# Cross-shaped window attention on one core: 34 squares by VectorE's f16 product, and a new mix of tile kinds

## The chip, the cores and the metric

One of the eight cores of a Trainium2 chip runs the kernel. Its engines work side by side, each from an instruction queue of its own, and wait for each other by semaphores: TensorE (PE) multiplies matrices into PSUM, ScalarE (ACT) and VectorE (DVE) read PSUM and SBUF, GpSimd (POOL) reads and writes SBUF, SyncE (SP) issues transfers. The metric is the time of one execution on the device in microseconds; less is better.

## The reference

An image x of 224 x 224 positions with 96 channels is projected to queries, keys and values. The first 48 channels attend within horizontal stripes of 8 rows (28 windows of 1792 tokens), the last 48 within vertical stripes of 8 columns (28 windows more). The two results side by side go through an output projection.

```python
qkv = jnp.einsum('bhwc,cd->bhwd', x, wqkv)
q, k, v = (qkv[..., :C].copy(), qkv[..., C:2 * C].copy(), qkv[..., 2 * C:].copy())
scale = C2 ** (-0.5)                              # C2 = 48
qh = q[..., :C2].reshape(B * nh, sw * W, C2)      # horizontal stripes; kh, vh alike
ah = _softmax(jnp.einsum('bqc,bkc->bqk', qh, kh) * scale, axis=-1)
oh = jnp.einsum('bqk,bkc->bqc', ah, vh).reshape(B, H, W, C2)
...
# qv, kv, vv: the other 48 channels in vertical stripes, ov likewise
o = jnp.pad(oh, ...) + jnp.pad(ov, ...)
return jnp.einsum('bhwc,cd->bhwd', o, wo)
```

## The kernel before, in words

**Tiles.** The 56 windows are worked off in 28 pairs P, 14 horizontal and then 14 vertical; the two windows of a pair lie in the two halves of the 128 partitions. A pair's 1792 queries are cut into four chunks c (512, 512, 512 and 256). The keys go along the partitions. One tile is 128 x 1024 scores: 1024 columns are two blocks of 64 keys by 512 queries, for two windows (in the last chunk four blocks by 256 queries). There are 14 tiles for each chunk of 512 and 7 for the last, 49 for a pair, 1372 in all. A tile's scores come from `score_half` (L768: four matmuls of 512 columns, or eight of 256), its exponentials are written as 16-bit words into one of 33 buffers PT, and `pv_fn` (L791) multiplies these with the values and adds the products up in a PSUM bank. The first product uses the diagonal 64 x 64 quadrants of the PE array and the second the other two, so matmuls of the two run side by side in pairs.

**Kinds.** Four engines share the exponentials, and the table KINDS says for each P and c what kind its last tiles are:

- E (not written in the table): ScalarE takes the exponential of the whole tile out of two PSUM banks (L947, `emit_qk`).
- Q, two passes: VectorE makes a f16 word from the low 16 bits of the scores, in two halves (L1037, `emit_p`, "p1"); GpSimd squares the whole tile (L1046, `squared`, kind "T"); PE computes the scores a second time into other banks, and VectorE adds score and square to the word whose bits are a bf16 (L1039, "f").
- H, four words: VectorE makes one word from the scores with one addition, in two halves (L1035), and GpSimd makes three shifted copies of it in three further PT buffers (L1051, `shifted`, kind "S"). All four words are multiplied with values, the three copies with values that GpSimd weighted before (V2, L1056), so an H tile costs four products L791 where the other kinds cost one.

Q and H tiles use a ring of four PSUM banks, together with the projections' results; E tiles use two fixed sets of two banks.

**Order.** The order of PE's work is written out by hand in ORDER, a string of letters for each P: q is scores and exponential of an E tile, 1 and x the two halves of a Q or H tile's first scores, 2 and y those of the second scores (3 both halves of a first one), v one product with the values, k, f, g and j parts of projections. While the program is built, a planner walks through these letters with a cost for each operation (D_H, D_SQ, D_AF and so on, in us) and decides from them in which order VectorE (`dve_step`) and GpSimd (`pool_step`) take the work that is ready. What it decides is fixed in each engine's queue; at run time semaphores alone hold an instruction back. VectorE also empties all projections and finished sums out of PSUM (L599, L608, L643, L711, L967), and GpSimd also normalises (L1022) and weights the values.

The lines of the three steps of a Q tile:

```python
lambda e: e.tensor_scalar(y.bitcast(FP16), l, YA ** 0.5 / 65536.0, -YA ** 0.5 * YD, ALU.mult, ALU.add)  # p1
return ("T", D_SQ, lambda e: e.tensor_tensor(y, y, y, ALU.mult), yk + ["pser"], yk)                      # squared
lambda e: e.scalar_tensor_tensor(y.bitcast(U16), f, QK, y.bitcast(FP16), ALU.add, ALU.add)               # f
```

Of the kernel before, what the change touches and what calls it, by code (L numbers as in the profile page):

```python
# [12 lines left out]
ALU = mybir.AluOpType  # L13
# [3 lines left out]
PHASE = 192.5  # L17
YA, YD = 43.12396, 0.0085264
QK, HK = -8394.91455, 5086.5133 + 128.0 * (85.205091 - 192.5)
SHIFTS = [32, 64, 96]  # L20
# [3 lines left out]
    ["QHH", "HHQQ", "QH", ""],  # L24
    ["HQQH", "HQ", "HQQHQ", ""],
    ["QHHHQQ", "HQQQ", "QQH", ""],
    ["HHQH", "QQ", "HQQHQQH", ""],
    ["HQHQQQH", "Q", "HHQH", ""],
    ["QHQQQ", "HQHQQ", "HQHHQQ", ""],
    ["HHQQQ", "QQQQ", "QH", ""],  # L30
    ["HQQHQ", "HQ", "HHQ", ""],
    ["QQQHHQH", "QQQQQHH", "", ""],
    ["HQQQHH", "HQQQQH", "QHH", ""],
    ["Q", "HQQQHQ", "QHQ", ""],
    ["HHQQHQQ", "QQQQH", "H", ""],
    ["HQQHQQH", "QQQHH", "", ""],
    ["HQQQHQ", "HQQQHQ", "H", ""],
    ["HHQQQQQ", "QHQ", "HH", ""],
    ["HQHQQQH", "QQQ", "HH", ""],
    ["HQHQHQ", "HQQQ", "HQ", ""],  # L40
    ["HHQQ", "HQHQHQ", "QQ", ""],
    ["HHQHQQ", "HQ", "HHQQ", ""],
    ["HHQQH", "HQQ", "HHQ", ""],
    ["QHHQQ", "HQQHQQ", "H", ""],
    ["HQHQHQQ", "HQHQ", "QH", ""],
    ["HHQQHQ", "H", "HQQQHQ", ""],
    ["HHQHQ", "HQQHHQ", "", ""],
    ["HQQH", "QHHQHQ", "QH", ""],
    ["HQHQQ", "H", "HHQQH", ""],
    ["QQHQHQ", "QHHQQH", "Q", ""],  # L50
    ["QHQHQH", "HQQQQ", "HH", ""],
# [10 lines left out]
SEMD, SEMP, SELF, SEMX = 0.14, 0.11, 0.19, 0.03  # L62
# [4 lines left out]
D_H, D_F, D_SQ, D_AF = 0.599, 1.132, 1.851, 1.01  # L67
D_AW, D_AG, D_TS = 2.088, 1.127, 0.009
# [11 lines left out]
    "qqkjkqjkqjkq1qxjq1qx1kqjkqjkjq2vxvqyvkqvjkvjq1vvxkqvjkvqjkvjq1vkvqjkvjvqxv1vqkvxvjq1vvqxv1vqvxvqkv1vqjv2qvvxvyqv1vqv2vyqvxvq2vvyqvkvqjvkqv1jvqvkxvqjkvjq1vkvqjvxvqv1xvqv2vkq",  # L80
    "vj1vqvvyqvxvqv1xvqvvkqjkvjqvk1vqjxvvqv1kqvjxvqv1vxvqkv2jqvyvv1qkvjqvx1vqvkvqvxjvqv1vqxvv1q2vvxqvyvqv2v1qvyvqxvvkqvjvqv12vqvyvqvxkvqjkvjqkv2qjvvyqvk1qj2vvqxv1vqxvq1vvyqvvqvx1vq",
    "xvqvv1xqvkjqvkvjqvk1vqjkvjqvxv2qvkvyjqv1vxqv2vvq1xvvq1vvyqkvjqxv2vqvkvqjyvqv2vqyvv1qvv2qvxv1qvvyqv2vyvq2vvqxvkqjkvqjkvjq1vxqvvyvqkv1vqxvjqv1xvqkvjqv1xvqv1vqvvxq1vvq",
    "vxv1qvxqvkvjq2vv1qvkvjqyvkvqjkvjqxv2vqkvyjvq2vv1qvyvqxv1vqvxvkqv1vjqvkvqjxvq12vqvyvqvk2qvxjvqvkyqjkvjqv12qvkvjqvvyqvvxqv2vvyq1vkqvjvxqvv3qvv1vqvxvq1vvxqv3vqv1vqvvxq",
    "v2vqvyv1qvvkvqjkvqjxvkvqj2vqvvykqvjv2qvvy1qvv2vqkvyjqvx1vvqvkxqvj1vqvkvqxjvvqv1qvxv2vq1vvqxvyvqv1qvxvkqvjkvqjkvqjkv1jqvxvq1vvkqvjxvq1vxvqv2vq1vvqxvvyqv1vqvxv1vq2vxqvqv1vyq",
    "xvqv2vyvqkjqv2vqkv1vjqkvjqkvyvjqv2vqxv1vqyvvxqv2vqkvyjvqv1vqkvxvqjvv1qvkxvqj2vqyvv1qvvxqv2vyqvv1qvvxkqvjkqjv2vqvykqvjkvqj1vkqvxvjq1vvqx1qvx1qvvxqv1xvq",
    "v2vqyvvqv2yq1vvxqvvqv1xvqv1vqxvvkqjkqjkvjq1vvxqvkvjq1vvxqkv2jqv1yvvq2vqvxvyqvv2yqvkjq2yvqvkvqjk2qjkqvjyvq2vkvqjyvqv2vyqvkvjq1vkvqvjxvq1vvqvv2qvxvyqv1vvqxv1vqxvvq1vxvqv3vq",
    "vvqv1vqxvv2qvvkyqjkvqjkvjq2vvkqv1jvqxvvyqv2vqkv1vjqxvv1qyvvkvqxvjqvkvqv2jvqyvvq1vvxqv1xvqv1vqxvv1qvvxq1vvkqvjkqjkxqjvkvqv1jq2vvkqjyqvvx2vqv1vqvyxvqvv1qvxv1qvvxq1vqvvxvq12qxvq",
    "yv2qvyvvqkvjqkv2jqvkvjq1vkvqjvyqvxvkvqj1vxvq2vyvqkvjqv2yvqv1vqv2vyqvvkqvj2vqvxvqyv1vqxvvqv21vqvxvq1vvyqvvxvq1vxvqvkqjv1qvkxvqj1vqvxvkqvjkvqjkvjq1vxqvv2vq1vvqyvxq",
    "vv1q2vvqvkxjqvkvjqyvkvqj2vvqkvyjqv1vqvxv1vqkvjxvq1vvxq1vkvqvxjqvv2vqyvkqjkvqj2vqvy2vqvv1qyvkvqjxvqv1vxqvkvjq2vkvqjyvvq1vvxqkvjqv1vqvxv1qvxvq2vvqv1yvqvvx1vqxvvq",
    "1vxvqv1vqvxvqv1vqv2yvqvvkqjkvjqxvkvqjkvjqv2yqv1vvqxv2qkjyqv12vqvvyqkvvjqvxvqv1xvqv1v2vqvyqv2vvxqyvvq1vxvqv1vqvxkvqjkqj1vq2vqyvkvqjkvxqjv1qvxvvq1kvqjvxvq1xqv1vkqvxvjqv1vqvxq",  # L90
    "v12vqyvvqvk2qjvkjqvyvxqvkvjqv2kvqjyvqv1vxvqkvj2qvyv1vqv2vqyv2vqyvxvqkvjqvkvqj2vqvyvq1vv2vqyxvqvv1qxvv1qvxvq1vvkvqjkqvjvxq1vkvqjkvjqvxvkqv1jvqvx1vqvxvqv2vq1xvqvv1qyvvq",
# [122 lines left out]
def bass_standalone__window_attn_cswin__vision_kernel(  # L214
# [28 lines left out]
    with es:  # L243
# [855 lines left out]
        def dve_step():  # L1099
# [52 lines left out]
            else:  # L1152
# [444 lines left out]
```

## Time and profile before

| | |
|---|---|
| median of 3 runs | 975.38 us (974.14 to 975.89) |
| the profiled execution | 976.11 us, span 974.3 us |
| busy, share of the span | PE 99%, ACT 98%, DVE 97%, POOL 96% |
| exponentials on ACT (L947) | 1031, mean 1047 ns |
| squares on POOL (L1046) | 192, mean 1895 ns |
| shifted copies on POOL (L1051) | 447, mean 1047 ns |
| matmuls L768 and L791 | 7064 and 8060 |

The span goes from the first instruction to the last; the rest of an execution's time lies around it. Busy time is the time in which at least one instruction of the engine ran, and consecutive instructions of one engine overlap a little. The ends of matmuls are modelled, so PE's busy share says less than its waits. A group's row gives line, engine, operation, output and inputs with shapes, count, then busy us and mean ns, then the engine's idle time before these instructions with what ended it.

### The profile page before, as it was taken

To read this page: it belongs to the slowest core of one execution; us is meant where nothing else is said; L and a number is where in the kernel's file an instruction comes from. 1 tells how busy PE (TensorE), PEld (TensorE's weight loads), DVE (VectorE), ACT (ScalarE), POOL (GpSimd) and SP (SyncE) were. 2 spreads that over 40 slices of the span, in tenths; PEclk is the share of its full clock that TensorE was granted. 3 is DMA by queue.
4 is the path that set the end of the run, shared out by engine and by line. 5 is a ranking of instruction groups with operands and counts; after the bars stand their busy time and mean duration, and the time that the engine had idled before them with its cause. 6 is when DMAs were issued, how large, how long until landed. Compare 5 with 4: busy or idle time off the path is not lost.

```text
span 974.3 us, 48091 instructions
## 1 busy us (share of the span) xinstructions
PE 963.4 (99%) x20945; PEld 625.9 (64%) x20945; DVE 943.7 (97%) x1803; ACT 957.5 (98%) x1044; POOL 934.4 (96%) x826
## 2 busy tenths in 40 slices
PE   9999999999999999999999999999999999999997
PEld 5666666565666566556666756666676676666665
DVE  6999999999999999999999999999999999999995
ACT  7999999999999999999999999999999999999997
POOL 6999999999999999999999999999899999999995
PEclk9999999999999999999999999999999999999999
DMA  9998559944974883523174376455625546554333
GB/s 189 164 186 135 82 92 163 143 86 85 159 119 67 130 117 55 78 50 64 17 112 76 72 116 115 69 96 107 119 58 108 106 77 92 97 101 88 73 76 75
DMA packets 429267, 97.82 MB, mean 100 GB/s; under 512 B 403648, under 2 KB 428832, under 8 KB 429056
## 3 DMA queue, kind: packets, MB, share of 16 engines
q1 hardware_dynamic: 427920, 93.57, 55.8%
q8 instruction: 164, 2.69, 1.2%
q0 software_dynamic: 448, 0.69, 0.2%
q10 hardware_dynamic: 688, 0.49, 0.2%
q14 instruction: 47, 0.39, 0.1%
HBM read 28.31 MB, written 28.21 MB: 58 GB/s over the span
## 4 chain that ended last, share of the span: by engine, by line
PE 89%; DVE 3%; ACT 3%; POOL 2%; issue 1%; POOLq 0%; DVEq 0%; ACTq 0%
PE ps L791 42%; PE ps L768 35%; PE ps L594 5%; PE ps L638 4%; ACT PT L947 3%; PE ps L705 3%; DVE PT L1037 1%; DVE PT L1039 1%; POOL PT L1046 1%; POOL PT L1051 1%; DVE KT_sb L599 1%; DVE PT L1035 0%; PE ps L424 0%; PE ps L815 0%; POOL ohn L1022 0%
## 5 line engine op out<-in xcount | busy, mean ns | idle before, releaser
L947 ACT ACTIVATE PT<-ps 128x1024 bf16<-128x1024 f32 x1031 | 951.3, 1047 | 7.4 <-PE ps L768 5.0
L791 PE MATMUL ps<-PT,V_sb 64*49 64x512 bf16 (+1 forms) x8060 | 877.4, 357 | 1.7 <-issue 1.4
L768 PE MATMUL ps<-QT_sb,KT_sb 49*64 49x512 bf16 (+2 forms) x7064 | 843.5, 359 | 1.8 <-DVE PT L1039 0.7
L1051 POOL TENSOR_SCALAR PT<-PT 128x1024 uint16<-128x1024 uint16 x447 | 456.3, 1047 | 8.8 <-DVE PT L1035 3.2
L791 PEld LDWEIGHTS ps<-PT,V_sb 64*49 64x49 bf16 x8060 | 378.2, 101 | 93.3 <-DVE PT L1039 2.1
L768 PEld LDWEIGHTS ps<-QT_sb,KT_sb 49*64 49x64 bf16 (+1 forms) x7064 | 309.4, 105 | 152.6 <-ACT PT L947 62.3
L1046 POOL TENSOR_TENSOR PT<-PT 128x1024 f16<-128x1024 f16 x192 | 360.0, 1895 | 8.6 <-DVE PT L1037 8.3
L1039 DVE SCALAR_TENSOR_TENSOR PT<-ps,PT 128x512 uint16<-128x512 f32 x384 | 252.8, 682 | 6.9 <-POOL PT L1046 3.4
L1037 DVE TENSOR_SCALAR PT<-ps 128x512 f16<-128x512 int16 x383 | 250.0, 684 | 3.0 <-PE ps L768 1.6
L1035 DVE TENSOR_SCALAR PT<-ps 128x512 uint16<-128x512 f32 (+1 forms) x296 | 197.1, 686 | 2.3 <-PE ps L768 1.6
L594 PE MATMUL ps<-xT_sb,wq_sb 64*64 64x512 bf16 (+4 forms) x446 | 78.2, 358 | 0.3
L638 PEld LDWEIGHTS ps<-w_sb,xT_sb 64*64 64x64 bf16 (+1 forms) x3136 | 66.8, 109 | 15.6 <-PE ps L638 2.8
L594 PE MATMUL ps<-xT_sb,w_sb 64*64 64x512 bf16 (+4 forms) x446 | 73.9, 357 | 0.5 <-DVE PT L1039 0.2
L638 PE MATMUL ps<-w_sb,xT_sb 64*64 64x48 bf16 (+1 forms) x3136 | 72.1, 186 | 0.0
L967 DVE CAST OT_sb<-ps 113x512 bf16<-113x512 f32 x111 | 68.6, 618 | 2.4 <-PE ps L791 2.2
L608 DVE CAST QT_sb<-ps 128x512 bf16<-128x512 f32 (+1 forms) x111 | 67.6, 614 | 0.5 <-PE ps L768 0.2
L599 DVE TENSOR_SCALAR_CACHE_REDUCE KT_sb<-ps 128x512 bf16<-128x512 f32 x108 | 64.3, 617 | 0.3 <-PE ps L768 0.2
L705 PE MATMUL ps<-wo,oc_all 33*64 33x96 bf16 (+1 forms) x1568 | 61.1, 204 | 0.6
L705 PEld LDWEIGHTS ps<-wo,oc_all 33*64 33x64 bf16 (+1 forms) x1568 | 49.5, 106 | 17.1 <-PE ps L705 3.0
L643 DVE CAST V_sb<-ps 128x480 bf16<-128x480 f32 (+1 forms) x84 | 50.4, 616 | 0.7 <-PE ps L638 0.3
L711 DVE CAST og<-ps 128x480 bf16<-128x480 f32 x81 | 49.6, 617 | 1.2 <-PE ps L672 0.5
L1056 POOL TENSOR_SCALAR V_sb<-V_sb 128x294 bf16<-128x294 bf16 x84 | 37.2, 443 | 7.6 <-DVE V_sb L643 0.7
(67 smaller groups left out, 223.6 us busy)
## 6 DMA issues: line engine op xcount, KB each, us to landing
xT_sb<-xt_dram SPq DMA_DIRECT2D x28, 336.0 KB, 5.6
xp_dram<-in_x_dram SPq DMA_DIRECT2D x26, 336.0 KB
oc_all<-xp_dram SPq DMA_DIRECT2D x26, 336.0 KB, 3.9
xt_dram<-xT_sb SPq DMA_DIRECT2D x26, 336.0 KB, 6.4
out_dram<-og SPq DMA_DIRECT2D x179, 48.0 KB, 2.2
oh_all<-ohn SPq DMA_DIRECT2D x52, 84.0 KB, 3.0
stg<-oh_all SPq DMA_DIRECT2D x13, 336.0 KB, 4.7
xt_dram<-xT_sb SPq DMA_DIRECT2D x4, 168.0 KB, 4.6
```

Source lines behind the costliest of these rows:

```text
L594: ins = e.matmul(bk[64 * w:64 * w + 64, 0:qs], lhsT=lw, rhs=xT_sb[b][a:z, 1 - w, q0:q0 + qs], start=part != 1, stop=part != 0)
L599: return e.tensor_scalar(KT_sb[b][:, q0:q0 + qs], bk[:, 0:qs], alpha, None, ALU.mult, ALU.add, accum_out=ksum[b][:, k_i[P, c]:k_i[P, c] + 1])
L638: ins = e.matmul(bk[64 * w:64 * w + 64, j * C2:(j + 1) * C2], lhsT=xT_sb[b][a:z, 1 - w, t0:t0 + 64], rhs=w_sb[a:z, wblk(P, "v"), 0:C2], st ...
L705: ins = e.matmul(bk[64 * h:64 * h + 64, s * C:(s + 1) * C], lhsT=oc_T[b][a:z, 4 * (m // 2) + 2 * h + m % 2, :].rearrange("c (t u) -> c u t ...
L768: ins = e.matmul(bk[p0:p0 + 64, i * qs:(i + 1) * qs], lhsT=KT_sb[b][p0:p0 + nr, kb * 64:kb * 64 + 64], rhs=QT_sb[b][p0:p0 + nr, t["q0"]:t[ ...
L791: ins = e.matmul(bank(pb)[p0:p0 + CA, 0:qs], lhsT=V2_sb[b][wi][r0:r0 + 64, kb - 2 * NKT + NVB[wi], :] if z else V_sb[b][r0:r0 + 64, kb, :] ...
L947: S.commit("act", 0.0, D_ACT, None, lambda e, s=s, slot=slot: e.activation(PT[slot][:], ps[:, 512 * SETS[s]:512 * SETS[s] + 1024], ACTF.Ex ...
L1035: fn, reads, writes = lambda e: e.tensor_scalar(y.bitcast(U16), f, HK, None, ALU.add), bk, ptk
L1037: fn, reads, writes = lambda e: e.tensor_scalar(y.bitcast(FP16), l, YA ** 0.5 / 65536.0, -YA ** 0.5 * YD, ALU.mult, ALU.add), bk, ptk
L1039: fn, reads, writes = lambda e: e.scalar_tensor_tensor(y.bitcast(U16), f, QK, y.bitcast(FP16), ALU.add, ALU.add), bk + ptk, ptk
L1046: return ("T", D_SQ, lambda e: e.tensor_tensor(y, y, y, ALU.mult), yk + ["pser"], yk)
L1051: return ("S", D_AF, lambda e: e.tensor_scalar(w1, w0, 1.0, float(sh), ALU.mult, ALU.add), pt_keys(tl["slot"]) + ["pser"], pt_keys(tl["slo ...
```

## The change

KINDS is a new table: 134 tiles of kind Q instead of 192, 180 of kind H instead of 149, and 34 of a new kind D; 1024 tiles are left to ScalarE instead of 1031. A D tile goes the way of a Q tile, but its square is an instruction of VectorE, a product of the whole f16 tile with itself in SBUF, put into VectorE's queue after the tile's first pass. It has one PT buffer, as Q has. ORDER is new for every P. The planner has a cost for the product (D_SQD) and for the gap to a following instruction on the same tile (SELFD). In VectorE's choice among ready work the product ranks with the first and second passes, behind the emptying of finished sums and projections.

```diff
 KINDS = [
-    ["QHH", "HHQQ", "QH", ""],
-    ["HQQH", "HQ", "HQQHQ", ""],
+    ["QHH", "HHH", "HQQHQD", ""],
+    ["QHQH", "QQ", "QQQHH", ""],
...
+D_SQD, SELFD = 0.60, 0.19
...
 ORDER = [
-    "qqkjkqjkqjkq1qxjq1qx1kqjkqjkjq2vxvqyvkqvjkvjq1vvxkqvjkvqjkvjq1vkvqjkvjvqxv1v...
+    "qqkjkqjkqjkq1xj1qxqk1xq2qjykjkqjqkvvjqv1vqxv1vqvxkvqjv1vkqjxvq1vvxqvk1vqjkvj...
...
-        ends = [("QH", 1, PHASE)]
+        ends = [("QHD", 1, PHASE)]
...
-        two_pass = [t for t in p_seq if t["kind"] == "Q"]
+        two_pass = [t for t in p_seq if t["kind"] in "QD"]
...
-            return ("T", D_SQ, lambda e: e.tensor_tensor(y, y, y, ALU.mult), yk + ["pser"], yk)
+            return ("T", D_SQ, lambda e: e.tensor_tensor(y, y, y, ALU.mult), yk + (["pser"] if tl["kind"] == "Q" else []), yk)
...
-                    key = {"ot": -1e6, "p1": 1e5 + d["ready"], "f": 1e5 + d["ready"]}.get(d["what"], d["ready"])
+                    key = {"ot": -1e6, "p1": 1e5 + d["ready"], "sq": 1e5 + d["ready"], "f": 1e5 + d["ready"]}.get(d["what"], d["ready"])
...
+            elif what == "sq":
+                tl = d["tl"]
+                m = squared(tl)
+                S.commit("dve", 0.0, D_SQD, D_SQD + SEMD, m[2], m[3], m[4])
+                tl["mid_t"] = st + d["dur"] + SELFD
+                tl["ready2"] = True
...
-                if tl["nh"] == 2 and what == "p1" and tl["kind"] == "Q":
+                if tl["nh"] == 2 and what == "p1" and tl["kind"] == "D":
+                    dq.append(dict(what="sq", tl=tl, ready=st + d["dur"] + SELFD, dur=D_SQD))
+                elif tl["nh"] == 2 and what == "p1" and tl["kind"] == "Q":
...
-                    if tl["kind"] == "Q":
+                    if tl["kind"] in "QD":
                         return
...
-                tl["slots"] = [slot_free.pop(0) for _ in range(1 if tl["kind"] == "Q" else 1 + len(SHIFTS))]
+                tl["slots"] = [slot_free.pop(0) for _ in range(1 if tl["kind"] in "QD" else 1 + len(SHIFTS))]
...
-            if tl["kind"] in "EQ" or slot != tl["slot"] or "w1" in tl:
+            if tl["kind"] in "EQD" or slot != tl["slot"] or "w1" in tl:
```

More of the change, by code (lines that the diff above doesn't have):

```diff
@@ L23 @@
 KINDS = [
-    ["QHH", "HHQQ", "QH", ""],
-    ["HQQH", "HQ", "HQQHQ", ""],
[L26 to L51, printed above, removed]
+    ["QHH", "HHH", "HQQHQD", ""],
+    ["QHQH", "QQ", "QQQHH", ""],
+    ["HQQHQH", "HH", "D", ""],
+    ["QHDHHQQ", "HQHH", "D", ""],
+    ["HQHDQH", "HHQDQH", "HQQ", ""],
+    ["HHQHQ", "HQQH", "HDH", ""],
+    ["HDHQHQQ", "Q", "HHHQD", ""],
+    ["HHQHQQ", "HQ", "HHQQHDQ", ""],
+    ["HHH", "HQQQD", "HHH", ""],
+    ["HDQHHQ", "QQHQH", "HQHQ", ""],
+    ["DQHH", "HHDQHQ", "HDQ", ""],
+    ["HQHH", "HQQQH", "HQH", ""],
+    ["HDQHHQ", "HQQHHQQ", "H", ""],
+    ["HDH", "QQQHH", "DHHHQQ", ""],
+    ["QHQHQ", "QHDH", "HH", ""],
+    ["HDHH", "DDHQ", "QHHQH", ""],
+    ["HQHQQHQ", "HH", "HQQ", ""],
+    ["QQHH", "H", "HDHHDQ", ""],
+    ["HHQDH", "HQQ", "HHHQ", ""],
+    ["QHQQH", "H", "HDHQHQD", ""],
+    ["HHHD", "QHHQQH", "H", ""],
+    ["QHQQHH", "QQHHHQD", "", ""],
+    ["HHQHQQ", "H", "QHHHD", ""],
+    ["H", "QHHQQHQ", "HHQ", ""],
+    ["QHQQHQH", "H", "HDHDH", ""],
+    ["HQQQ", "HHHQQ", "HQHD", ""],
+    ["HHQQHQ", "HQHH", "D", ""],
+    ["HQHQQH", "QHHQQ", "HQH", ""],
 ]
```

56 lines of the change are left out of this document (28 added, 28 removed).

## The prediction

> **What bounds the kernel now.** I read the busy shares first, then stretches of 50 us, then the groups by shape, the waits, and the timeline for the true step of each operation.
>
> The page's busy row, and rows of the stretches (us, then PE, weight load, VectorE, ScalarE, GpSimd busy):
>
> ```profile
> PE 963.4 (99%) x20945; PEld 625.9 (64%) x20945; DVE 943.7 (97%) x1803; ACT 957.5 (98%) x1044; POOL 934.4 (96%) x826
> ```
> ```profile
> 0.00:50.00 50.00, 48.83 (x928) 31.57 (x930) 41.80 (x90) 44.48 (x52) 40.03 (x60) 1.00 0.92 175
> ...
> 100.00:150.00 50.00, 49.92 (x1072) 32.90 (x1070) 49.35 (x88) 49.83 (x55) 49.34 (x45) 1.00 0.54 89
> ...
> 750.00:800.00 50.00, 50.00 (x1210) 35.58 (x1208) 49.46 (x94) 50.00 (x55) 49.07 (x45) 1.00 0.48 87
> ...
> 950.00:974.00 24.00, 19.25 (x437) 14.29 (x428) 14.40 (x48) 18.88 (x23) 13.04 (x19) 0.96 0.31 77
> sum 974.00, PE 963.38 PEld 625.91 DVE 943.68 ACT 957.50 POOL 934.44; mean PE 48.17 PEld 31.30 DVE 47.18 ACT 47.87 POOL 46.72
> ```
>
> Take the first and last row off the sum and 900 us of middle remain. There ScalarE is busy 957.50 - 44.48 - 18.88 = 894.1, idle 5.9. VectorE is busy 887.5, idle 12.5 (and 8.2 + 9.6 = 17.8 idle at the two ends). GpSimd is busy 881.4, idle 18.6. So three engines are full within 2%, ScalarE first, VectorE only 6.6 us behind it. PE's 99% says little, since its ends are modelled; the waits say more:
>
> ```profile
> PEld ps L768 <- ACT PT L947: 62.3, 237, 0.6
> ...
> ACT PT L947 <- PE ps L768: 5.0, 12, 1.4
> ```
> ```profile
> DVE PT L1039 <- POOL PT L1046: 3.4, 8, 0.9
> ```
>
> PE stands 62.3 us at score matmuls because ScalarE has not yet freed the banks; ScalarE waits for those matmuls only 5.0 us. ScalarE paces the kernel, and time should fall with its work for as long as VectorE, GpSimd and PE can follow.
>
> **The change part by part.** The groups that it touches (count, then busy us, mean ns):
>
> ```profile
> L947 ACT ACTIVATE PT<-ps 128x1024 bf16<-128x1024 f32 x1031 | 951.3, 1047 | 7.4 <-PE ps L768 5.0 <-PE ps L791 1.0 <-DVE wq_sb L626 0.3
> L791 PE MATMUL ps<-PT,V_sb 64*49 64x512 bf16 x6492 | 782.4, 378 | 1.5 <-issue 1.4
> ...
> L1051 POOL TENSOR_SCALAR PT<-PT 128x1024 uint16<-128x1024 uint16 x447 | 456.3, 1047 | 8.8 <-DVE PT L1035 3.2 <-PE ps L791 2.2 <-POOL PT L1051 0.6
> ...
> L1046 POOL TENSOR_TENSOR PT<-PT 128x1024 f16<-128x1024 f16 x192 | 360.0, 1895 | 8.6 <-DVE PT L1037 8.3 <-PE ps L791 0.3
> L1039 DVE SCALAR_TENSOR_TENSOR PT<-ps,PT 128x512 uint16<-128x512 f32 x384 | 252.8, 682 | 6.9 <-POOL PT L1046 3.4 <-PE ps L791 2.0 <-PE ps L768 0.9
> ...
> L1035 DVE TENSOR_SCALAR PT<-ps 128x1024 uint16<-128x1024 f32 x2 | 2.4, 1220 | 0.0
> ```
>
> Before: 1031 tiles by ScalarE, 192 of two passes (kind Q), 447/3 = 149 of four words (kind H), together 1372. After: 134 Q, 34 D and 180 H, so 1372 - 348 = 1024 for ScalarE. Neighbouring instructions overlap, so their mean duration is not what one more costs. The step is, from unbroken runs in the timeline (start, length, count):
>
> ```profile
> 299.52 18.48 ACT L947 ACTIVATE PT<-ps 128x1024 bf16<-128x1024 f32 x20
> ```
> ```profile
> 601.91 2.47 DVE L1037 TENSOR_SCALAR PT<-ps 128x512 f16<-128x512 int16 x4
> ```
> ```profile
> 604.74 5.60 POOL L1046 TENSOR_TENSOR PT<-PT 128x1024 f16<-128x1024 f16 x3
> 610.30 6.10 POOL L1051 TENSOR_SCALAR PT<-PT 128x1024 uint16<-128x1024 uint16 x6
> ```
> ```profile
> 336.49 0.38 PE L791 MATMUL ps<-PT,V_sb 64*49 64x512 bf16 x2
> ...
> 337.79 0.38 PE L791 MATMUL ps<-PT,V_sb 64*49 64x512 bf16 x2
> ```
>
> An exponential steps at (18.48 - 1.05)/19 = 0.917 us, a VectorE half tile at (2.47 - 0.68)/3 = 0.597, a GpSimd square at (5.60 - 1.90)/2 = 1.85, a GpSimd shift at (6.10 - 1.05)/5 = 1.01, a pair of 512-column matmuls of the second product at (337.79 - 336.49)/6 = 0.217 (seven such pairs).
>
> ScalarE: 7 exponentials fewer, 7 x 0.917 = **6.4 us less**. They lie on the pacing engine, so all of it counts.
>
> GpSimd: 58 squares fewer (-107.3), 31 x 3 = 93 shifts more (+93.9): 13 us less. Off the pace, taken as nothing. The 34 D tiles also no longer wait for GpSimd; the wait of 3.4 us in all shows there is next to nothing to win.
>
> VectorE, without the product: half tiles were 192 x 4 + 149 x 2 = 1066 and become 168 x 4 + 180 x 2 = 1032, 34 fewer: -20.3 us. The product itself, 34 whole tiles, f16 in and out, both operands the same SBUF tile, stands in no row. Low end 0.597: a half tile reads 512 f32 words, as many bytes per partition as 1024 f16 words. High end: one element per cycle as in the 1024-wide row, 1.22 - 0.08 overlap = 1.14, plus whatever the product has to wait for. A gain below the low end is excluded: no DVE row of that many bytes is shorter. I take 0.60, since by bytes the half tile is the nearest row: +20.4. VectorE then stands where it stood, 943.8 us.
>
> The Trainium skill ("VectorE: DVE Perf Modes", The perf-mode tier table) puts a 16-bit product of two SBUF tensors at two elements per cycle; an estimate from its 2048-wide figure is 0.69 us in duration, which would leave the sum as it is. No run here shows that yet.
>
> Is 943.8 still hidden? With its 17.8 us of idle ends and a middle as tight as ScalarE's (5.9), VectorE needs 943.8 + 17.8 + 5.9 = 967.5 of span; ScalarE, 6.4 less than now, 974.3 - 6.4 = 967.9. It fits by 0.4 us: the cover is gone. Every further microsecond on VectorE is a microsecond of time, or, counted at today's span, VectorE can take 12.5 - 5.9 = 6.6 us more, **0.19 us for each of 34 products**, before the change stops paying.
>
> New waits: the product waits for the tile's own first pass on VectorE, and the second pass for the product. Behind them in VectorE's queue are projection evictions and other tiles' half tiles, whose banks PE waits for. The planner (SELFD = 0.19) puts other work into the gap; if neither gap were filled, 34 x 2 x 0.19 = 13 us would be added. I take 0, because unbroken strings of ready VectorE work are the rule (49.46 busy of 50).
>
> PE: 93 more value products, 24 fewer score passes (192 - 168), each of 4 matmuls of 512 columns: +372 and -96. The value side of the array grows by 186 pairs x 0.217 = 40 us, the score side shrinks by 10. That the array can do it is read from the stretches, value products alone:
>
> ```profile
> 0.00:50.00 50.00, 29.98 (x275) 12.75 (x277) 1.00 0.92 175
> ...
> 100.00:150.00 50.00, 46.89 (x446) 20.72 (x444) 1.00 0.54 89
> ...
> 750.00:800.00 50.00, 47.79 (x452) 21.43 (x448) 1.00 0.48 87
> ...
> 950.00:974.00 24.00, 17.14 (x171) 9.88 (x166) 0.96 0.31 77
> ```
>
> 8060 before, less the two ends, is 423 per 50 us; after it must be (8432 - 446)/894 x 50 = 447 on average. Stretches of 446 and 452 are in the trace, one with the most PE instructions of any 50 us but one (1210), and ScalarE was 49.83 and 50.00 busy in them. So at this rate PE need not delay ScalarE. But it has to hold everywhere: low end 0, high end a doubling of ScalarE's middle idle, +5.9. I take +1.0, near the two rows. A four-word tile also holds four of the 33 word buffers PT until PE has read them, and there are 31 such tiles more; the shift row above waits for PE 2.2 us in all, so buffers are not short now and I take 0. DMA and SP work is unchanged in number; its place in the order changes with the plan, taken as nothing: ScalarE's row names no transfer among its releasers.
>
> Sum: the profiled execution took 976.1 us (974.3 span and 1.8 around it); 976.1 - 6.4 + 0.1 + 1.0 = 970.8. The median of the runs lies 0.7 below that execution: **970.0**.
>
> **The rivals.** First, on the other side: the product has to wait for GpSimd. It would read SBUF through both of its operands while GpSimd reads SBUF without a break. For it speaks that the trace has no VectorE instruction with two SBUF tensors in the steady state, so nothing shows that the two can run together; against it, that in a 50 us stretch at 49 us busy both engines hold their durations with one SBUF operand on VectorE. The price, if a product must let the current GpSimd instruction finish: after the change GpSimd spends 180 x 3 x 1.01 = 545 us in shifts (mean rest 0.51), 134 x 1.85 = 248 in squares (0.93) and some 118 in other work (0.4): (545 x 0.51 + 248 x 0.93 + 118 x 0.4)/969 = 0.57 us, three times the 0.19 from which it decides. VectorE becomes 943.8 + 34 x 0.57 = 963.2, and the span 963.2 + 17.8 + 0 to 5.9 = 981 to 987: about **985**, 1% slower. GpSimd would lose up to 34 x 0.6 = 20 us the other way round, which its 13 us less and 18.6 idle cover.
>
> This is a rule of the Trainium skill ("SBUF — State Buffer", Who interferes with whom): a VectorE instruction with two SBUF inputs and a GpSimd instruction that reads SBUF exclude each other for a whole instruction. By it the time is this rival's, not the forecast's; no run here shows it so far, as no such pair occurs.
>
> Second: the product runs at one element per cycle, 1.14 us: 34 x 0.54 = 18 more on VectorE, span 980 to 986, about **983**. Against it the narrow words; for it, that every VectorE row shown above runs at that rate.
>
> Third: PE, with the value side at 447 of some 452 per 50 us, delays ScalarE by the high end: 969.0 + 5.9, about **975**, no change.
>
> **How the numbers follow.** Forecast 0.48; waiting for GpSimd 0.36; one element per cycle 0.05; PE 0.11. The forecast alone spans 967.5 to 972.5 (PE term 0 to 3, ends of the run 1 either way). The range takes in the first rival nearly whole: 967.5 to 988. A measurement of this kernel tells about 0.2%, 2 us, from no change (the runs lie 1.75 apart). Faster: 0.46 of the forecast and 0.03 of the PE case, 0.49. Same: 0.02 + 0.06 and 0.03 of short waits near 0.19 us, 0.11. Slower: the rest, 0.40.
>
> **What would show it.** 1024 exponentials, still stepping 0.917 and idle some 6 us in the middle; 540 shifts, 134 squares on GpSimd; 34 VectorE products of about 0.68 us mean whose followers start 0.6 later. Products of 1.2 us would be either rival: all alike means the rate, scattered between 0.7 and 2.5 and ending with GpSimd's instructions means the wait; then ScalarE's waits for PE and PE's for VectorE grow. Shifts longer than 1047 ns mean that GpSimd pays. The prediction is wrong if VectorE's middle idle goes to nothing while ScalarE's grows past 10 us.

## The result and the profile after

The changed kernel takes **1029.08 us** (median; runs 1026.49 to 1035.64) against 974.44 us (973.59 to 975.89) of the kernel before, run beside it. The ratio is 1.0569 with a 95% interval of [1.0538, 1.0599]: 54.6 us slower, where 5 us less was forecast. It lies outside the range; the rival that made a product wait for GpSimd named the mechanism and had 985 us. Line numbers of the changed kernel are one higher than before (exponentials L948, scores L769, value products L792, both sorts of square L1047, shifts L1052).

Page of the changed kernel, span and busy row:

```profile
span 1029.7 us, 48585 instructions
...
PE 980.6 (95%) x21221; PEld 658.5 (64%) x21221; DVE 994.2 (97%) x1804; ACT 956.9 (93%) x1036; POOL 928.6 (90%) x862
```

Busy time on ScalarE and GpSimd stayed within 6 us of before; VectorE's rose by 50.5 us, from 943.7 to 994.2. Stretches of 50 us of the changed kernel (columns as before; the last three are the granted clock, the DMA share and GB/s):

```profile
0.00:50.00 50.00, 46.53 (x843) 27.63 (x847) 42.45 (x87) 41.52 (x49) 38.71 (x65) 1.00 0.87 169
...
250.00:300.00 50.00, 41.59 (x804) 27.16 (x798) 48.07 (x69) 38.28 (x42) 40.64 (x36) 0.90 0.60 92
...
1000.00:1029.00 29.00, 25.76 (x546) 19.48 (x544) 20.20 (x62) 23.79 (x27) 19.98 (x25) 0.96 0.24 67
sum 1029.00, PE 980.62 PEld 658.51 DVE 994.17 ACT 956.91 POOL 928.62; mean PE 46.70 PEld 31.36 DVE 47.34 ACT 45.57 POOL 44.22
```

Without its first and last row ScalarE is busy 956.91 - 41.52 - 23.79 = 891.6 of 950 us: idle 58.4 in the middle, where it was idle 5.9. From 250 to 300 us it runs 42 instructions where it ran 55. VectorE looks full, yet runs only 69 instructions in those 50 us, where it ran 95. The groups by shape say which of them grew:

```profile
L948 ACT ACTIVATE PT<-ps 128x1024 bf16<-128x1024 f32 x1024 | 951.2, 1042 | 63.8 <-PE ps L769 47.5 <-PE ps L792 9.1 <-PE ps L595 4.8
L1052 POOL TENSOR_SCALAR PT<-PT 128x1024 uint16<-128x1024 uint16 x540 | 556.7, 1057 | 22.7 <-DVE PT L1036 5.9 <-PE ps L792 4.7 <-PE ps L769 4.1
L1047 POOL TENSOR_TENSOR PT<-PT 128x1024 f16<-128x1024 f16 x134 | 252.2, 1896 | 15.2 <-DVE PT L1038 10.2 <-PE ps L792 4.8
L1047 DVE TENSOR_TENSOR PT<-PT 128x1024 f16<-128x1024 f16 x34 | 74.9, 2205 | 0.0
```

The counts are the announced ones (1024, 540, 134, 34). A shift takes 1057 ns in the mean where it took 1047. The 34 products take 2205 ns each on average. The view of that line (minimum, median, maximum in ns) shows that this is no rate:

```profile
L1047 DVE TENSOR_TENSOR PT<-PT x34: 679/1468/6975, 38.2 to 970.5; 128x1024 f16<-128x1024 f16 x34
```

An undisturbed product is 0.68 us, the longest 6.98. Over the 34 records the time beyond 0.68 adds up to 51.8 us. The waits show who pays (who waits, for whom, us in all, times, longest):

```profile
ACT PT L948 <- PE ps L769: 47.5, 37, 6.6
PEld ps L769 <- ACT PT L948: 37.8, 156, 0.6
POOL V_sb L1057 <- DVE V_sb L644: 27.1, 14, 4.2
PEld ps L769 <- DVE V_sb L644: 21.8, 15, 5.9
PE ps L769 <- DVE V_sb L644: 16.5, 4, 5.4
...
DVE PT L1040 <- POOL PT L1047: 5.9, 3, 5.4
```

ScalarE's wait for scores was 5.0 us and is 47.5; PE's wait for ScalarE, the sign that ScalarE paces, fell from 62.3 to 37.8. PE and GpSimd now wait for L644, the copy of V out of PSUM, which can stand in VectorE's queue behind a product; GpSimd's wait for this copy was 0.7 us before. In the chain that ended last VectorE has 16% (it had 3%), the products alone 5%:

```profile
PE 77%; DVE 16%; issue 3%; POOL 3%; ACT 1%; DMA 0%; SPq 0%; POOLq 0%; DVEq 0%
```

Two products in the timeline (start, us, engine, line; a row joins neighbours of one kind). The first three rows are GpSimd about the longest product, the next three VectorE there; the last two are GpSimd and VectorE about a common one:

```profile
286.79 1.05 POOL L1052 TENSOR_SCALAR PT<-PT 128x1024 uint16<-128x1024 uint16 x1
287.80 3.75 POOL L1047 TENSOR_TENSOR PT<-PT 128x1024 f16<-128x1024 f16 x2
291.51 3.07 POOL L1052 TENSOR_SCALAR PT<-PT 128x1024 uint16<-128x1024 uint16 x3
...
287.54 0.68 DVE L609 CAST QT_sb<-ps 128x512 bf16<-128x512 f32 x1
288.14 6.97 DVE L1047 TENSOR_TENSOR PT<-PT 128x1024 f16<-128x1024 f16 x1
295.04 0.65 DVE L644 CAST V_sb<-ps 128x480 bf16<-128x480 f32 x1
...
335.32 2.49 POOL L1052 TENSOR_SCALAR PT<-PT 128x1024 uint16<-128x1024 uint16 x2
335.78 1.12 DVE L1047 TENSOR_TENSOR PT<-PT 128x1024 f16<-128x1024 f16 x1
```

At 335.78 the product meets a shift that ends near 336.4, goes in behind it and ends at 336.90; the next shift is held up, so two shifts take 2.49 us and not 2.06. At 288.14 it is passed over at four boundaries, by a square and three shifts, and ends 0.53 us after GpSimd's last instruction (291.51 + 3.07 = 294.58; 288.14 + 6.97 = 295.11). The profile puts the 4.79 us that GpSimd then stands idle down to PE, and PE had stood 5.40 us for L644, which waits behind the product (in brackets: the idle time before, and what ended it):

```profile
299.36 1.89 POOL L1047 TENSOR_TENSOR PT<-PT 128x1024 f16<-128x1024 f16 x1 [4.79 <-PE ps L792]
...
295.74 0.63 PE L769 MATMUL ps<-QT_sb,KT_sb 51*64 51x512 bf16 x2 [5.40 <-DVE V_sb L644]
```

Of the 34 products 23 go in at the first chance (0.68 to 2.20 us, together 12.7 us of waiting, 0.55 each). Eleven are passed over at one or more boundaries (2.11 to 6.98 us), always until GpSimd has nothing to run; they hold 39.1 of the 51.8 us. Behind each of the eleven GpSimd stands idle for 1.1 to 4.8 us; behind six of them its next work is L1057, the weighted copies of V, which waits for L644.

What such a stop does to PE, in steps of 5 us:

```profile
285.00:290.00 5.00, 5.00 (x154) 3.56 (x146) 5.00 (x7) 5.00 (x6) 5.00 (x5) 1.00 0.92 175
290.00:295.00 5.00, 0.34 (x6) 0.00 (x0) 5.00 (x1) 1.24 (x2) 4.58 (x4) 0.79 1.15 176
295.00:300.00 5.00, 4.26 (x44) 3.11 (x48) 4.08 (x8) 1.88 (x2) 0.64 (x1) 0.53 0.13 18
300.00:305.00 5.00, 5.00 (x118) 3.69 (x110) 5.00 (x9) 4.79 (x6) 3.27 (x3) 1.00 0.02 3
```

PE runs 6 matmuls in 5 us, ScalarE dries up behind it, and when VectorE is free again the granted clock is 0.53 for the next stretch. Over the whole run it is 0.984 (before 0.999).

### The profile page after: what moved, and what is told of

Its sections match the earlier page's. It is cut to its first block, busy times and chain, and to the rows that moved or that the text cites. A ratio compares the mean times of both kernels' runs of the same rounds, so it can differ in the third digit from the quotient of the medians.

```text
span 1029.7 us, 48585 instructions
## 1 busy us (share of the span) xinstructions
PE 980.6 (95%) x21221; PEld 658.5 (64%) x21221; DVE 994.2 (97%) x1804; ACT 956.9 (93%) x1036; POOL 928.6 (90%) x862
## 4 chain that ended last, share of the span: by engine, by line
PE 77%; DVE 16%; issue 3%; POOL 3%; ACT 1%; DMA 0%; SPq 0%; POOLq 0%; DVEq 0%
PE ps L792 38%; PE ps L769 29%; DVE PT L1047 5%; PE ps L595 4%; DVE PT L1038 3%; PE ps L639 3%; DVE PT L1036 3%; PE ps L706 2%; DVE PT L1040 2%; POOL PT L1052 1%; POOL PT L1047 1%; ACT PT L948 1%; DVE QT_sb L609 1%; DVE V_sb L644 1%; DVE KT_sb L600 1%
## 5 line engine op out<-in xcount | busy, mean ns | idle before, releaser
L948 ACT ACTIVATE PT<-ps 128x1024 bf16<-128x1024 f32 x1024 | 951.2, 1042 | 63.8 <-PE ps L769 47.5
L792 PE MATMUL ps<-PT,V_sb 64*49 64x512 bf16 (+1 forms) x8432 | 918.5, 360 | 5.8 <-DVE PT L1040 5.1
L769 PE MATMUL ps<-QT_sb,KT_sb 49*64 49x512 bf16 (+2 forms) x6968 | 843.8, 362 | 28.3 <-DVE V_sb L644 16.5
L1052 POOL TENSOR_SCALAR PT<-PT 128x1024 uint16<-128x1024 uint16 x540 | 556.7, 1057 | 22.7 <-DVE PT L1036 5.9
L792 PEld LDWEIGHTS ps<-PT,V_sb 64*49 64x49 bf16 x8432 | 413.7, 102 | 107.5 <-DVE PT L1040 6.3
L769 PEld LDWEIGHTS ps<-QT_sb,KT_sb 49*64 49x64 bf16 (+1 forms) x6968 | 310.1, 106 | 153.0 <-ACT PT L948 37.8
L1047 POOL TENSOR_TENSOR PT<-PT 128x1024 f16<-128x1024 f16 x134 | 252.2, 1896 | 15.2 <-DVE PT L1038 10.2
L1036 DVE TENSOR_SCALAR PT<-ps 128x512 uint16<-128x512 f32 x359 | 238.5, 681 | 4.0 <-PE ps L769 2.0
L1040 DVE SCALAR_TENSOR_TENSOR PT<-ps,PT 128x512 uint16<-128x512 f32 x336 | 222.7, 679 | 9.1 <-POOL PT L1047 5.9
L1038 DVE TENSOR_SCALAR PT<-ps 128x512 f16<-128x512 int16 x334 | 217.8, 683 | 2.6 <-PE ps L769 1.2
L595 PE MATMUL ps<-xT_sb,w_sb 33*64 33x512 bf16 (+4 forms) x446 | 71.8, 357 | 3.4 <-DVE OT_sb L968 3.0
L1047 DVE TENSOR_TENSOR PT<-PT 128x1024 f16<-128x1024 f16 x34 | 74.9, 2205 | 0.0
L1057 POOL TENSOR_SCALAR V_sb<-V_sb 128x294 bf16<-128x294 bf16 x84 | 37.1, 442 | 32.9 <-DVE V_sb L644 27.1
L609 DVE CAST QT_sb<-ps 128x512 bf16<-128x512 f32 (+1 forms) x111 | 66.2, 609 | 0.5 <-PE ps L595 0.2
L706 PE MATMUL ps<-wo,oc_all 64*64 64x96 bf16 (+1 forms) x1568 | 60.5, 204 | 1.0 <-DVE PT L1036 0.5
L644 DVE CAST V_sb<-ps 128x480 bf16<-128x480 f32 (+1 forms) x84 | 50.7, 614 | 1.7 <-PE ps L639 1.4
```

What stands on the lines that cost most here:

```text
L595: ins = e.matmul(bk[64 * w:64 * w + 64, 0:qs], lhsT=lw, rhs=xT_sb[b][a:z, 1 - w, q0:q0 + qs], start=part != 1, stop=part != 0)
L609: return e.tensor_copy(QT_sb[b][:, q0:q0 + qs], bk[:, 0:qs])
L706: ins = e.matmul(bk[64 * h:64 * h + 64, s * C:(s + 1) * C], lhsT=oc_T[b][a:z, 4 * (m // 2) + 2 * h + m % 2, :].rearrange("c (t u) -> c u t ...
L769: ins = e.matmul(bk[p0:p0 + 64, i * qs:(i + 1) * qs], lhsT=KT_sb[b][p0:p0 + nr, kb * 64:kb * 64 + 64], rhs=QT_sb[b][p0:p0 + nr, t["q0"]:t[ ...
L792: ins = e.matmul(bank(pb)[p0:p0 + CA, 0:qs], lhsT=V2_sb[b][wi][r0:r0 + 64, kb - 2 * NKT + NVB[wi], :] if z else V_sb[b][r0:r0 + 64, kb, :] ...
L948: S.commit("act", 0.0, D_ACT, None, lambda e, s=s, slot=slot: e.activation(PT[slot][:], ps[:, 512 * SETS[s]:512 * SETS[s] + 1024], ACTF.Ex ...
```

## The experiments

Theory: a VectorE product of two SBUF inputs and a GpSimd instruction that reads SBUF exclude each other (called the lock below), and the waits make the loss. Rivals: the new plan is slow even with undisturbed products (PE, the order, more VectorE work); or the product is slow in itself. Each ratio is to the kernel before, run beside on the same chip.

**The product replaced by a write (e1_memset).**

```
- S.commit("dve", 0.0, D_SQD, D_SQD + SEMD, m[2], m[3], m[4])
+ S.commit("dve", 0.0, D_SQD, D_SQD + SEMD,
+          lambda e, w=PT[tl["slot"]][:].bitcast(FP32): e.memset(w, 1.0), m[3], m[4])
```

> The changed kernel with each of the 34 products replaced at its place by a VectorE memset of 512 f32 words over the same tile (so these tiles are not squared): the same length when alone (about 0.6 us a step), the same waits, no SBUF input. Theory 1 (the product waits for the shared way into SBUF until GpSimd's unbroken run of instructions ends): the plan itself is sound, 970 us, 968 to 974, memsets 0.68 us each. Theory 2 (a wait for one GpSimd instruction only, the rest of the loss is the new plan): 1029 less 34 x 0.6 = about 1010. Theory 3 (the new mix and order, with 93 more value products on PE, costs the time): above 1020.

Measured 979.86 us, ratio 1.0039 [1.0026, 1.0053]: 49 of the 54.6 us are gone when VectorE only writes in the same place of the same order. But it is not faster than before. The write lasted 0.485 us, and 0.6 was planned. Busy row of its page, and a wait of its stretch from 450 to 500 us:

```profile
PE 964.5 (99%) x21221; PEld 657.7 (67%) x21221; DVE 938.9 (96%) x1804; ACT 953.0 (97%) x1036; POOL 920.8 (94%) x862
```
```profile
POOL ohn L1023 <- DMA oh_all<-ohn: 5.9, 1, 5.9
ACT PT L948 <- PE ps L769: 6.7, 3, 5.3
```

GpSimd stood once for 5.9 us for a transfer out of the row buffer `ohn`, and ScalarE lost 5.3 us there: one cost of the new order that has nothing to do with the product (the changed kernel has this wait too, 6.6 us, and the kernel before has none).

**GpSimd held until the product is done (e2_hold).** The next GpSimd instruction in the plan also waits for the product's end, so GpSimd can't pass a product more than once:

```
+ S.hold = ("dve", S.cnt["dve"])              # behind the product's commit
+ if eng == "pool" and self.hold:             # in commit
+     d.add(self.hold); self.hold = None
```

> The changed kernel; the GpSimd instruction that comes next in the plan after each product also waits for that product's end. Theory 1: a product now waits for at most the instruction that runs (mean rest about 0.57 us, longest 1.9), mean length 1.2 to 1.3 instead of 2.2 us, and the time falls by some 34 us to 990 to 1000. Theory 2: products had no more than one instruction to wait for, so nothing is won and GpSimd only loses: 1029 to 1040. Theory 3: no change, 1029.

Measured 997.08 us, ratio 1.0214 [1.0197, 1.0231]: one more wait on GpSimd makes the kernel 32 us faster than the changed one. The products in it:

```profile
L1051 DVE TENSOR_TENSOR PT<-PT x34: 672/1246/2260, 38.1 to 936.6; 128x1024 f16<-128x1024 f16 x34
```

The longest is 2.26 us, and the time beyond 0.68 adds up to 18.3 us, 0.54 each. Being passed over costs 32 us, net of what the hold costs GpSimd. The other 22 us hold the waits for one instruction and whatever else the new plan costs; later runs take them apart.

**GpSimd squares all 168 tiles, same order (e3_dq).** In the list of kinds every D becomes a Q.

> The changed kernel with its 34 D tiles made Q tiles, so that GpSimd squares all 168; the same order of PE's work. Theory 1: GpSimd becomes the bound with 920.9 + 34 x 1.85 = 984 us of work and 21 of idle ends, 1000 to 1010, still faster than with the products on VectorE. Theory 2: the same, since the plan is at fault only in part: 1010 to 1020. Theory 3: the order is at fault and GpSimd's load comes on top: above 1040.

Measured 1053.86 us, ratio 1.0806 [1.0787, 1.0825]; 1000 to 1010 was expected, a miss. I had counted load only (GpSimd is busy 983.8 us). In an order planned for early squares they come late, and VectorE waits for them in its queue:

```profile
ACT PT L948 <- PE ps L769: 62.1, 39, 7.5
...
DVE PT L1040 <- POOL PT L1047: 39.3, 19, 7.7
```

So this run shows that this order does not bear its 34 squares on GpSimd; it does not show what the products cost.

**The pair by itself (m1_lock).** Products against runs of GpSimd instructions, in a small kernel:

```
+ shifts(8, w)       # GpSimd: 8 of e.tensor_scalar(dst[j], src, 1.0, 32.0, ALU.mult, ALU.add)
+ wait_memset(0, w)  # VectorE: a write of 0.5 us, then
+ product(3)         #   e.tensor_tensor(yy[3], yy[3], yy[3], ALU.mult)
```

> A small kernel that leaves out the whole computation and writes zeros: VectorE products (128 x 1024 f16, one SBUF tile times itself) and other VectorE instructions beside runs of GpSimd instructions that are queued without a wait between them. Theory 1: alone 0.68 us; issued 0.6 us into a run of 1, 2, 4, 8 shifts, a product ends about 0.55 us after the run: about 1.0, 2.0, 4.0, 8.0 us long; beside four squares about 7.4 us; where each shift waits for the one before, about 1.0 us; memsets and instructions with one PSUM and one SBUF input stay at 0.68. Theory 2: never longer than one GpSimd instruction and itself, 1.6 us beside shifts and 2.5 beside squares. If only reads are shared, a product beside GpSimd memsets is 0.68 us; a shift that comes during a run of products would show whether VectorE's run holds GpSimd off in the same way (over 3 us) or for one product (under 1.7).

Alone, three products take 1.90 us, 0.63 each. A product that came about 0.5 us after a run of shifts had begun went in at once, in 0.63 us, and the run paid 0.97: eight shifts beside writes of VectorE, the row below, took 8.10, beside a product 9.07. With one input in PSUM the VectorE instruction left the run alone (8.11).

```profile
46.08 8.10 POOL L67 TENSOR_SCALAR dst<-src 128x1024 uint16<-128x1024 uint16 x8 [0.16 <-POOL dst L90]
```

**e1 with a second row buffer (e4_memset_ohn2).** `ohn` becomes two buffers, used in turn, with a semaphore each; the product is still the write.

```
- dst = ohn[:, k0:k1, :, :].rearrange("p k w c -> p (k w) c")
+ dst = ohn[b][:, k0:k1, :, :].rearrange("p k w c -> p (k w) c")
```

> The memset version again (the 34 tiles are not squared), and GpSimd's normalised rows go alternately into two buffers (the second one in og, which is free in that half), each with its own semaphore, so that the normalisation no longer waits for the transfer that empties the buffer (5.9 us of GpSimd at 483 us of the span, with 5.3 us of ScalarE idle behind it). If that wait is where the plan lost its gain: 972 to 975. If it is PE, with 93 more value products, that takes it back everywhere: 978 to 980, as without the edit.

Measured 975.5 us, ratio 1.0005 [0.9994, 1.0015]: the transfer wait was worth 4.4 us, and the rest is even with the kernel before, though ScalarE has 7 exponentials less. Its busy row, and its exponentials:

```profile
PE 962.9 (99%) x21221; PEld 656.7 (67%) x21221; DVE 939.8 (97%) x1804; ACT 953.1 (98%) x1036; POOL 920.7 (95%) x862
```
```profile
L949 ACT ACTIVATE PT<-ps 128x1024 bf16<-128x1024 f32 x1024 | 947.3, 1042 | 11.5 <-PE ps L793 4.9 <-PE ps L770 4.5 <-PE ps L596 0.3
```

Busy fell by 4.0 us (951.3 to 947.3), idle ahead of them rose by 4.1 (7.4 to 11.5): given back in full. PE's wait for ScalarE is 39.7 us here, so its fall from 62.3 in the changed kernel came with the new plan and not with the products.

**A slot for each product (e5_reserve).** With the two row buffers the planner puts a product off to the planned end of GpSimd's current instruction and starts nothing on GpSimd until it is done:

```
+ if d["what"] == "sq" and not d.get("go"):
...
+     tm["rsv"] = True
+     dq.append(dict(d, go=True, ready=max(t, tm["pool"])))
```

> The real products, with the two row buffers, and a planner that knows the lock: a product that is ready is put off until the GpSimd instruction that runs is planned to end, GpSimd starts nothing until it is done, and VectorE takes other work meanwhile. Theory 1 (lock until a gap in GpSimd's work): products of 0.7 to 0.9 us in the mean, GpSimd gives up 34 x 0.8 = 27 us which it has (921 + 27 + 21 of ends = 969): 973 to 982, with a chance to be even with the kernel before. Theory 2 (the product is slow beside GpSimd in any case): products stay above 1.2 us, 990 or more.

Measured 1004.31 us, ratio 1.03 [1.0285, 1.0315], outside the expected time, while the products came out as expected: 25 of the 34 take under 0.9 us,

```profile
L1052 DVE TENSOR_TENSOR PT<-PT x34: 676/685/1472, 38.2 to 945.3; 128x1024 f16<-128x1024 f16 x34
```

but the work that is put off no longer meets the order of the tiles. GpSimd stands 12.7 us for the words of H tiles (longest 8.5) and 12.6 for products, VectorE 11.7 for squares, and ScalarE's wait for scores is 24.4.

**The old plan with 34 D tiles (e7_old_plan_d).** Kinds and order of the kernel before, 34 of its 192 Q made D, for example:

```
+ ["HQDH", "HQ", "HQQHQ", ""],
+ ["QHHHDQ", "HQQQ", "DQH", ""],
```

> The kernel before, its own table and order, with 34 of its 192 Q tiles (every sixth or so) made D tiles: the product alone, without the new mix. VectorE gains 34 x 0.6 = 20 us of work, GpSimd loses 63. Theory 1: VectorE is the bound at 943.7 + 20.4 + 17.8 = 982 even without waits, and GpSimd, less loaded by 63 us, has more gaps, so waits of 0.5 to 1.0 us each: 1000 to 1020. Theory 2 (one instruction's rest, 0.57 us): 1000 at most. If the loss came with the new plan: 985.

Measured 1007.77 us, ratio 1.0337 [1.0319, 1.0354]:

```profile
PE 974.5 (97%) x20945; PEld 627.2 (62%) x20945; DVE 979.6 (97%) x1837; ACT 962.4 (96%) x1044; POOL 880.7 (88%) x792
```
```profile
L1047 DVE TENSOR_TENSOR PT<-PT x34: 683/1018/2455, 45.7 to 975.1; 128x1024 f16<-128x1024 f16 x34
```

Here VectorE gets 34 x 0.6 = 20.4 us more and no half tiles less, and 17.9 us of waiting, 0.53 each; only one product of 34 is passed over. GpSimd is busy 53.7 us less than before and the time does not fall: the span grows by 31.0 us and VectorE's busy time by 35.9.

**Runs with other neighbours (m2_lock, m3_lock).** The small kernel again, first with products in the middle of runs of 4, 8 and 16 shifts, then with the waits and neighbours of the changed kernel about them, up to

```
+ shifts2(8, w, mix)      # each shift waits for something long done; mix: two squares first
+ pre(w, d, own, cast)    # two first passes, a copy out of PSUM, a product that waits for its own engine
```

> A small kernel as the first one (leaves out the whole computation), but the products are issued 2 us into a run of GpSimd instructions, when it is in full swing. In the first one a product issued 0.5 us after the run's first start went at once and cost the run 0.96 us. Theory 1: beside runs of 4, 8, 16 shifts (4.1, 8.1, 16.2 us) a product ends 0.5 us after the run: about 2.5, 6.5 and 14.7 us long; beside 4 squares about 6. With the fifth shift waiting for the product: 2.5, as with 4. Three products beside 8 shifts: the first 6.5, the others 0.68. Theory 2: 1.1 to 1.6 us beside shifts of any number. GpSimd memsets (write only): 0.68 if only the way for reads is shared. Where each shift waits for the one before: one shift's rest, under 1.7. A 16-bit copy of one input: as the product, if it uses the shared way too.

> A third small kernel (leaves out the whole computation). Open: in the changed kernel some products wait for one GpSimd instruction and some for four or five, until GpSimd's run ends; in the second small kernel all waited for one, with a run that was queued without waits. Six groups of three products, 1 to 2 us into a run of 8 instructions: shifts that wait on a semaphore met long ago; product that waits for its own engine; both; both behind two first passes and a copy out of PSUM; the same against two squares and six shifts; the same with transfers of 1.2 MB each in the background. The group in which products take 4 us and more (to the end of the run) has what makes the difference. If the form of the instructions decides, it is one of the first five; if transfers do, the sixth alone; if neither, all stay at 0.7 to 2.5 us and the cause is open.

In m2_lock each such product took 0.95 us, whatever the length of the run, and a run of eight 8.54:

```profile
20.47 8.54 POOL L67 TENSOR_SCALAR dst<-src 128x1024 uint16<-128x1024 uint16 x8 [0.16 <-POOL dst L67]
...
23.12 0.95 DVE L63 TENSOR_TENSOR yy<-yy 128x1024 f16<-128x1024 f16 x1
```

Beside GpSimd writes, which read nothing, it took 0.63 and the writes 7.20, as without it. In m3_lock the 18 products took 0.63 to 1.52. No product was passed over, in no group: the small kernels show the lock for one instruction, not what happens eleven times in the changed kernel.

**The write at the planned length (e6_memset_long).** e4 and a second write of 224 words for each D tile, so that VectorE gives up the planned 0.6 us:

```
+ S.commit("dve", 0.0, 0.0, SEMD, lambda e, w=pad[:, :]: e.memset(w, 0.0), [], [("pad",)])
```

> As the memset version with two row buffers (975.5 us), with a second memset of 224 words behind each first one, so that VectorE gives up 0.6 us for each of the 34 tiles, as planned, not 0.4 (these tiles are not squared). If VectorE is the second bound, as the sum had it, 7 us more work on it cost 2 to 6 us: 977 to 981. If PE's order sets the pace of this plan: 975.5, no change.

Measured 979.42 us, ratio 1.003 [1.0019, 1.004]: the change at the price that I had planned, without any contention and without the transfer wait. It is 0.3% slower than before.

```profile
PE 963.4 (99%) x21221; PEld 655.7 (67%) x21221; DVE 943.8 (97%) x1838; ACT 954.1 (98%) x1036; POOL 921.9 (94%) x862
```

**e2 with the two row buffers (e8_hold_ohn2).**

> The real products, the next GpSimd instruction held until each product ends, and two row buffers. Both losses are then cut as far as a wait can: 997 less the 4.4 us that the second buffer brought the memset version, 991 to 994. If the two are not separate (the hold already moves GpSimd off that transfer): 997.

Measured 993.36 us, ratio 1.0172 [1.0154, 1.019], as expected; products of 1266 ns mean. Against e6 it is 13.9 us: the price of real products that wait for one GpSimd instruction each (42.9 us busy, 19.8 of it beyond 0.68).

```profile
PE 973.0 (98%) x21221; PEld 652.9 (66%) x21221; DVE 961.2 (97%) x1804; ACT 957.8 (97%) x1036; POOL 925.7 (93%) x862
```

**What makes a product lose its turn (m4_lock, e9_gap).** Six of the seven products of the changed kernel that come right behind L609, the copy of Q out of PSUM, are passed over. m4_lock adds ScalarE and PE traffic to the small kernel; e9_gap puts a tiny write ahead of each product of the changed kernel:

```
+ S.commit("dve", 0.0, 0.0, 0.0, lambda e: e.memset(gap[:], 1.0), [], ["gap"])
```

> A small kernel; the whole computation is left out. Twelve VectorE f16 products of 128x1024, each behind two half-tile passes and a copy out of PSUM, meet an unbroken run of GpSimd instructions at three phases (behind 2, 3 or 4 memsets). Group G has ten ScalarE exponentials of 128x1024 from PSUM to SBUF beside it, group H 36 matmuls, I both, J both against two squares and six shifts. Theory 1 (the wait is for GpSimd's current instruction whatever ScalarE and PE do): all products 0.7 to 1.7 us (to 2.5 in J), runs of 8 shifts 8.5. Theory 2 (traffic of ScalarE or PE on SBUF makes a waiting product lose its turn, which the earlier small kernels did not have and the changed kernel has): products of 3 to 8 us that end with GpSimd's run in G and I, or in H and I.

> The changed kernel with one tiny VectorE write (128x8 f32, no input) ahead of each of the 34 products, same order of everything else. In the changed kernel 6 of the 7 products that come right behind the copy of a projection out of PSUM wait for GpSimd's whole run. If it is this neighbour that makes a product lose its turn, the write takes away some six waits of 3 to 6 us and costs 34 x 0.1 = 3 us: 1005 to 1015. If the neighbour doesn't matter: 1027 to 1036, and the products still reach 4 us and more behind these copies. If a small shift in time is enough to change which products lose their turn, some other products are long, and the time is between.

In m4_lock the twelve products took 0.77 to 1.52 us, for instance 1.31 in a full run beside exponentials, so traffic of the two engines isn't it. e9_gap measured 1029.59 us, ratio 1.0559 [1.0527, 1.0592], as the changed kernel; ten of its eleven places are passed over again, and no other:

```profile
281.22 0.68 DVE L610 CAST QT_sb<-ps 128x512 bf16<-128x512 f32 x1
281.84 7.55 DVE L1048 TENSOR_TENSOR PT<-PT 128x1024 f16<-128x1024 f16 x1
281.86 0.07 DVE L1157 MEMSET gap<- 128x8 f32 x1
```

The write's record of 0.07 us lies inside the waiting product's, so a write as the instruction directly ahead changes nothing; whether a longer gap would was not tried. The long products belong to their places in the order, not to chance. Why GpSimd passes a product there, and in no small kernel, stays open.

## Why the prediction was wrong

The counts and the product's own price came out. "I take 0.60" for the product: 0.679 us in duration at best in the changed kernel and 0.63 a step alone, so the rival of one element per cycle (1.14) is out. By the Trainium skill ("VectorE: DVE Perf Modes", The perf-mode tier table) 0.69 had been estimated; the trace agrees with its 0.68.

**The step that failed first** is the one that left the wait for GpSimd out of VectorE's sum: +20.4 became +20.4 and 51.8 us of waiting. "Every further microsecond on VectorE is a microsecond of time" was right. Span less VectorE's busy time, lock waits counted as busy, stays between 26 and 36 us over these kernels:

| kernel | span, us | VectorE busy | difference |
|---|---|---|---|
| before | 974.3 | 943.7 | 30.6 |
| e4, write of 0.485 us | 973.4 | 939.8 | 33.6 |
| e6, the same and a second write | 975.7 | 943.8 | 31.9 |
| e8, held, two row buffers | 990.9 | 961.2 | 29.7 |
| e2, held | 995.9 | 960.6 | 35.3 |
| e7, old plan | 1005.3 | 979.6 | 25.7 |
| e9, tiny writes | 1024.9 | 990.7 | 34.2 |
| after | 1029.7 | 994.2 | 35.5 |

Left out are the three with another wait in the way: e1 (39.4, the transfer), e5 (53.1, its order) and e3 (122.9, squares from GpSimd).

**The rival's size.** I priced a product's wait at a mean rest of the current instruction, 0.57 us. That is what the products pay that do wait for one instruction: 0.55 (23 of the changed kernel), 0.54 (e2), 0.53 (e7), 0.58 (e8). What was not thought of is that GpSimd can start the next instruction, and the one after, ahead of the waiting product. This took the mean to 51.8/34 = 1.52 us, and e2, which forbids it, gets 32 us back. The sign of it was given: scattered durations that end with GpSimd's instructions, then growing waits of ScalarE for PE and of PE for VectorE. The forecast left this mechanism out, the rival had it at a chance of 0.36, and the range, which took in the rival nearly whole, had no worse case of it. Longer shifts were named as the sign that GpSimd pays; they are 10 ns longer, 5 us in 540. The Trainium skill ("SBUF — State Buffer", Who interferes with whom) has this lock, with the pair held for one whole instruction by whoever issues first; the small kernels agree in that a product took 0.63 us alone or beside GpSimd writes and 0.95 behind one shift. They differ where a product that came 0.5 us after a run's first shift went in ahead of it; and for the eleven products that several later instructions pass, issue order does not decide either. There the trace stands. The chance of 0.48 for a product without any wait was too high.

**The step that failed second** is "They lie on the pacing engine, so all of it counts". With no contention at all the -6.4 us did not come: e4 is even, e6 is 3.0 us above the kernel before run beside it. The sum of VectorE counted on its middle idle shrinking from 12.5 to 5.9, ScalarE's measure, a span of VectorE busy + 23.7. No run got there; so 943.8 meant about 975, not 967.5. From e4 to e6 VectorE alone gets more work, 4.0 us, and the time rises by 2.4 us by the ratios (3.9 between the medians): in the new order VectorE, not ScalarE, is the tight engine, and ScalarE's shorter work became idle time (e4: 4.0 less busy, 4.1 more idle). Which of the two paces the kernel before was not tried.

**Smaller steps.** "Its place in the order changes with the plan, taken as nothing": one wait for the row transfer, 4.4 us (e1 against e4). PE: +1.0 was not refuted; e4 ran all 8432 value products with ScalarE idle 11.5 us ahead of exponentials, of which 9.4 for PE, within the high end of +5.9 over the 6.0 of before. GpSimd's 13 us less, "taken as nothing", fits e7, which took 54 us off GpSimd and lost 32. The sum's 970.8 less 0.7 is 970.1, not 970.0, which changes nothing. The last sentence, that VectorE's middle idle goes to nothing, was not seen: it rose from 12.5 to 950 - (994.17 - 42.45 - 20.20) = 18.5, of which one wait for a late square of GpSimd is 5.4.

Of the 54.6 us, the step from the changed kernel to e2 is 32.0 (being passed over), from e2 to e8 3.7 (the transfer; 4.4 from e1 to e4), from e8 to e6 13.9 (waiting for one instruction), and from e6 to the kernel before, run beside it, 3.0 (what is left of the new plan). These add up to 52.7; the last 2.0 us lie between the medians of the kernel before in the two sets of runs, 974.4 and 976.4. The lower clock (0.984; e2 has 0.998) went away with the passing-over, so what it cost lies in the 32; how much that is was not tried.

## What to carry to other kernels

Before moving an elementwise product of two SBUF tensors to VectorE, look whether GpSimd reads SBUF beside it: price not only the current GpSimd instruction but the whole run up to GpSimd's next stop, and who is queued behind. If the product must be there, make GpSimd's next instruction wait for it: that was worth 32 us here, though the kernel stayed slower than before. When several engines are full within 2%, don't credit work taken off one of them; add each engine's idle time of today to its new busy time, and the largest sum is the forecast. Here that is VectorE's 943.8 + 30.6 = 974.4 us, and e6, with that busy time and no contention, has a span of 975.7; it is one case, worked out after the fact.

## What the runs showed of the hardware

- A waiting product can be passed over by four back-to-back GpSimd instructions (6.98 us), in e9_gap by five (7.55); in the changed kernel products are passed over in 11 of 34 places, and not once in the 30 tries of m3_lock and m4_lock with like waits, neighbours and traffic.
- A product of 0.63 us costs GpSimd's run about 0.4 when it goes in between two shifts (8.54 for eight shifts, 8.10 without it) and 0.97 when it comes early in the first.
- It is not a matter of two inputs alone: two 16-bit copies of one SBUF input each took 1.87 us together beside a run of shifts in m2_lock, and the run 8.44 where it is 8.10 beside writes. How long the copies take alone was not measured. GpSimd writes without an input don't contend (0.63 and 7.20).
- A PE that stood for some 5 us resumed at a granted clock of 0.53 in the next 5 us, and was at 1.00 again from 300 us on (changed kernel, 290 to 305 us).
